# Second pair's k on SyncE, the projection through GpSimd, and a fallback arm without VectorE, in a hash-attention kernel with a channel mix

## The chip, the cores and the metric

The kernel runs on one core of one Trainium2 chip. The metric is the device time of one execution in microseconds (us), as the median of several runs. A profile of one further execution shows what every engine did: PE (TensorE matmuls, with PEld for its weight loads), DVE (VectorE), ACT (ScalarE), POOL (GpSimd) and SP (SyncE, which here only issues transfers). A small q behind an engine's name, as in SPq, means that engine's sequencer: it issues a transfer, waits or branches.

## The reference

Attention comes first, on 4 batches of 8 heads, 768 positions, 64 values a head. Each position of q and k gets six bits, the signs of its products with a 64 x 6 projection; a query attends only to keys with the same six bits.

```python
q_bits = (np.einsum('bhsd,dk->bhsk', q, proj) > 0)
k_bits = (np.einsum('bhsd,dk->bhsk', k, proj) > 0)
mask = q_bucket[:, :, :, None] == k_bucket[:, :, None, :]
scores = np.where(mask, scale * np.matmul(q, k.transpose(0, 1, 3, 2)), -1e9)
attn = softmax(scores)                     # over the keys
x = np.matmul(attn, v)                     # heads side by side: (4, 768, 512)
```

The channel mix follows, with `x_prev` the sequence moved by one position:

```python
xk = mu_k * x + (1 - mu_k) * x_prev
xr = mu_r * x + (1 - mu_r) * x_prev
k = np.maximum(xk @ w_k, 0.0)              # 512 -> 1024
out = sigmoid(xr @ w_r) * ((k * k) @ w_v)  # 1024 -> 512
```

## The kernel before

The program has two arms. The fast arm computes everything under a bound on the size of the scores, and at its end `check_bound` writes an integer `flag` that says whether the bound held. All engines then load this flag (line 1127) and branch (line 1128): if it is zero, `general()` computes everything again in a slower and safer way. With the inputs here the flag holds, and every engine jumps over the general arm. Up to that branch each engine runs the fast arm in the order written in the kernel; a manual schedule keeps it.

The fast arm works on pairs of heads: 16 pairs, and 12 slots for each pair, two heads of six chunks of 128 keys. In each slot `score` (line 454) makes two matmuls, ScalarE takes the exponential (line 461), and two slots later `pv` multiplies the result with the values (lines 473 and 482). Between them stand matmuls of the channel mix (line 551), once a batch of attention is done. Tables named WORK and FETCH say what else is done in which slot.

The part that matters here is the start, before and in the first slots:

- `load_qk(0)` issues the two heads of pair 0's q from SyncE and k from ScalarE (line 249), and behind the first of each a copy of the projection into one half of the tile `projp` (line 254): rows 0 to 63 for one use, rows 64 to 127 for the other.
- A memset and a one-column exponential (line 685) make ScalarE load its table early.
- `load_v(0)` issues pair 0's values on SyncE (line 292), `load_qk(1)` pair 1's q on SyncE and its k on ScalarE (line 259). The second pair's values and pair 2's q and k come later on SyncE, then two small transfers for `mu` (line 721).
- `keep_warm` (line 692) issues matmuls on constants to `idle`, which nobody reads: 9 before the first real work of TensorE and 3 before the sign matmuls.
- `turn_pe` (lines 325 to 329) transposes one head's q or k on TensorE and copies it out of its bank on VectorE or ScalarE; `cast_pe` (lines 337 and 339) makes the bf16 copies for the scores, on GpSimd and ScalarE.
- `bits_first` (line 353) multiplies the projection with the turned q and k of pair 0, and VectorE takes the signs (line 384). Later pairs use `bits_pe` (line 395), whose signs go to their rows by SyncE transfers (line 405).
- `values` (lines 440 to 444) casts and sums values on GpSimd.

Four banks of PSUM go round between the transposes, the sign products and the outputs, by `take` and `give`. A transfer from SyncE or ScalarE signals one of eight semaphores in turn, and a transfer that would use one again waits for the earlier landing on it.

Of the kernel before, what the change touches and what calls it, by code (L numbers as in the profile page):

```python
# [16 lines left out]
P = 128  # L17
# [16 lines left out]
def kernel(  # L34
# [44 lines left out]
    def ffn_mix_unit(pools, b, dc, xt, ms):  # L79
        def u():  # L80
            x = xt[:, P : P + S]
            xp = xt[:, 0:S]
            nc.vector.memset(xt[:, 0:1], 0.0)
            nc.vector.tensor_copy(xt[:, 1:P], xt[:, S : S + P - 1])
            df = pools["df"].tile([P, S], BF16, name=f"df{b}_{dc}", tag="df")
            nc.vector.tensor_tensor(df, x, xp, op=ALU.subtract)
            for i, nm in enumerate(("xk", "xr")):
                m = pools["mix"].tile([P, S], BF16, name=f"{nm}{b}_{dc}", tag="mix")
                nc.vector.tensor_scalar(
                    out=m,  # L90
                    in0=df,
                    scalar1=mu_sb[:, i * NDC + dc : i * NDC + dc + 1],
                    scalar2=None,
                    op0=ALU.mult,
                )
                nc.vector.tensor_tensor(out=m, in0=m, in1=xp, op=ALU.add)
                ms[nm][dc] = m

        return u

    def ffn_k_unit(pools, b, fc, ms):
        def u():
            kp = pools["ps"].tile([P, 2, 512], FP32, name=f"kp{b}_{fc}", tag="sc")
            for dc in range(NDC):
                for sp in range(2):
                    nc.tensor.matmul(
                        kp[:, sp, 0:HALF],
                        wk_sb[:, dc, fc * P : (fc + 1) * P],
                        ms["xk"][dc][:, sp * HALF : (sp + 1) * HALF],
                        start=(dc == 0),  # L110
                        stop=(dc == NDC - 1),
                    )
            kr = pools["kr"].tile([P, 2, HALF], BF16, name=f"kr{b}_{fc}", tag="kr")
            if fc % 2:
                nc.scalar.activation(kr, kp[:, :, 0:HALF], AF.Relu, scale=ROOT_HALF)
            else:
                nc.vector.tensor_scalar(
                    out=kr, in0=kp[:, :, 0:HALF], scalar1=0.0, scalar2=ROOT_HALF,
                    op0=ALU.max, op1=ALU.mult,
                )  # L120
            k2 = pools["k2"].tile([P, 2, HALF], BF16, name=f"k2{b}_{fc}", tag="k2")
            nc.vector.tensor_tensor(out=k2, in0=kr, in1=kr, op=ALU.mult)
            ms["k2"][fc] = k2.rearrange("p s q -> p (s q)")

        return u

    def ffn_vr_unit(pools, b, c, ms):
        def u():
# [9 lines left out]
            for fc in range(NFC):  # L138
# [8 lines left out]
            th = pools["th"].tile([P, DM], BF16, name=f"th{b}_{c}", tag="th")  # L147
            nc.scalar.activation(th, vr[:, 1, :], AF.Tanh, scale=0.5)
            os_ = pools["os"].tile([P, DM], FP32, name=f"os{b}_{c}", tag="os")
            nc.vector.scalar_tensor_tensor(  # L150
                out=os_, in0=th, scalar=1.0, in1=vr[:, 0, :], op0=ALU.add, op1=ALU.mult
            )
# [16 lines left out]
    def fast():  # L169
        with ExitStack() as fx:  # L170
# [39 lines left out]
            KROWS = (slice(0, D + NB), slice(0, P))  # L210
            augs, vas, vss = [], [], []
            for s in range(NSET):
# [8 lines left out]
                for j in range(2):  # L221
                    nc.vector.memset(vas[s][j][:, :, D : D + 1], 1.0)
                    nc.vector.memset(vss[s][j][:, D : D + 1], float(NC_))

# [17 lines left out]
            def load_qk(n):  # L242
# [3 lines left out]
                if n == 0:  # L246
                    for j in range(2):
                        for i, eng in enumerate((nc.sync, nc.scalar)):
# [4 lines left out]
                            if j == 0:  # L253
                                eng.dma_start(
                                    out=projp[ROWS[i], NB * i : NB * i + NB], in_=proj
                                )
                    return
                for i, eng in enumerate((nc.sync, nc.scalar if n == 1 else nc.sync)):
                    eng.dma_start(
                        out=tl[:, i, :, :],  # L260
                        in_=SRC[i][b, 2 * t : 2 * t + 2].rearrange(
                            "j (p c) d -> p j (c d)", c=NC_
                        ),
                    )
# [123 lines left out]
            def bits_pe(n, js):  # L388

                groups = [(j, i) for j in js for i in range(2)]  # L390
                sg = sgp.tile([32 * len(groups), 2, HALF], BF16, name=f"sg{n}_{js[0]}", tag="sg2")
                for e in range(2):
                    which, bb = take([32 * len(groups), HALF], FP32, f"bb{n}_{js[0]}_{e}")
                    for g, (j, i) in enumerate(groups):
                        nc.tensor.matmul(
                            bb[32 * g : 32 * g + 32, :],
                            projp[ROWS[e], NB * e : NB * e + 32],
                            t32(n)[ROWS[e], i, j, :],
                            start=True,
                            stop=True,  # L400
                        )
                    signs(sg[:, e, :], bb)
                    give(which)
                for g, (j, i) in enumerate(groups):
                    nc.sync.dma_start(
                        out=augs[n % NSET]["qk"[i], j][SROWS[j], :],
                        in_=sg[32 * g : 32 * g + NB, :, :].rearrange("r e x -> r (e x)"),
                    )

            def bits_dve(n):  # L410

                which, bb = take([P, HALF], FP32, f"bb{n}")
                strips = [(e, i) for e in range(2) for i in range(2)]
                for g, (e, i) in enumerate(strips):
                    nc.tensor.matmul(  # L415
                        bb[32 * g : 32 * g + 32, :], projp[:, 0:32], t32(n)[:, i, e, :],
                        start=True, stop=True,
                    )
                sg = sgp.tile([P, HALF], BF16, name=f"sg{n}", tag="sg")
                signs(sg, bb)  # L420
                give(which)
                for j in range(2):
                    for g, (e, i) in enumerate(strips):
                        r = 32 * g + NB * j
                        nc.sync.dma_start(
# [259 lines left out]
            nc.scalar.activation(warm, warm, AF.Exp)  # L685
            load_v(0)
            load_qk(1)
# [12 lines left out]
            keep_warm(9, idle[:, 0, 0:HALF])  # L700
# [4 lines left out]
            keep_warm(3, idle[:, 0, 0:HALF])  # L705
# [10 lines left out]
            for i in range(2):  # L716
                cast_pe(0, i, 1, ((nc.gpsimd, nc.scalar), (nc.scalar, nc.gpsimd))[i])
            load_v(1)
            load_qk(2)
# [29 lines left out]
            def turn_mu():  # L749
# [29 lines left out]
                    lambda: bits_pe(1, (0, 1)),  # L779
# [14 lines left out]
                    lambda: bits_pe(2, (0, 1)),  # L794
# [17 lines left out]
                    lambda: bits_pe(3, (0, 1)),  # L812
# [211 lines left out]
    def general_head(nat, work, ps, xt, b, h, j):  # L1024
# [4 lines left out]
        for side, src in (("q", q), ("k", k)):  # L1029
# [10 lines left out]
            if side == "q":  # L1040
                nc.vector.tensor_copy(tv, tp[:, :, 0:HALF])
            else:
                nc.vector.tensor_scalar(
                    out=tv, in0=tp[:, :, 0:HALF], scalar1=0.125, scalar2=None, op0=ALU.mult
                )
            bp = ps.tile([NB, 2, 512], FP32, name=f"gbp{side}{id_}", tag="g2")
            for sp in range(2):
# [7 lines left out]
            nc.vector.tensor_scalar(  # L1055
                out=bt.rearrange("p (s q) -> p s q", s=2),
                in0=bp[:, :, 0:HALF],
                scalar1=0.0,
                scalar2=0.5,
                op0=ALU.is_gt,  # L1060
                op1=ALU.subtract,
            )
            tr[side], bits[side] = t, bt
        ob = work.tile([P, NC_, D], BF16, name=f"gob{id_}", tag="gob")
        for ic in range(NC_):
# [3 lines left out]
            for sp in range(2):  # L1069
# [8 lines left out]
            same = work.tile([P, 2, HALF], FP32, name=f"gsm{id_}_{ic}", tag="gsm")  # L1078
            nc.vector.tensor_scalar(
                out=same, in0=mp[:, :, 0:HALF], scalar1=1.25, scalar2=None, op0=ALU.is_gt  # L1080
            )
            neg = work.tile([P, 2, HALF], FP32, name=f"gng{id_}_{ic}", tag="gng")
            nc.vector.tensor_scalar(
                out=neg, in0=mp[:, :, 0:HALF], scalar1=1.25, scalar2=-1e9, op0=ALU.is_le, op1=ALU.mult
            )
            sm = work.tile([P, 2, HALF], FP32, name=f"gsc{id_}_{ic}", tag="gsc")
            nc.vector.tensor_tensor(out=sm, in0=sp_[:, :, 0:HALF], in1=same, op=ALU.mult)
            nc.vector.tensor_tensor(out=sm, in0=sm, in1=neg, op=ALU.add)
            mx = work.tile([P, 1], FP32, name=f"gmx{id_}_{ic}", tag="gmx")
            nc.vector.tensor_reduce(out=mx, in_=sm, axis=AX.XY, op=ALU.max, negate=True)  # L1090
            pe = work.tile([P, 2, HALF], FP32, name=f"gpe{id_}_{ic}", tag="gpe")
            den = work.tile([P, 1], FP32, name=f"gdn{id_}_{ic}", tag="gdn")
            nc.scalar.activation(pe, sm, AF.Exp, bias=mx, accum_out=den)
# [8 lines left out]
            nc.vector.tensor_copy(pt, tp[:, :, 0:HALF])  # L1102
            op_ = ps.tile([P, D], FP32, name=f"gop{id_}_{ic}", tag="g1")
            for c in range(NC_):
# [6 lines left out]
                )  # L1111
            rc = work.tile([P, 1], FP32, name=f"grc{id_}_{ic}", tag="grc")
            nc.vector.tensor_scalar(out=rc, in0=den, scalar1=1e-9, scalar2=None, op0=ALU.add)
            nc.vector.reciprocal(rc, rc)
            nc.vector.tensor_scalar(
                out=ob[:, ic, :], in0=op_, scalar1=rc, scalar2=None, op0=ALU.mult
            )
        ot = ps.tile([D, NC_, P], BF16, name=f"got{id_}", tag="g1")
        for c in range(NC_):
            nc.tensor.transpose(ot[:, c, :], ob[:, c, :], ident16)  # L1120
        nc.vector.tensor_copy(
# [38 lines left out]
```

## Time and profile before

| what | us |
|---|---|
| median of 3 runs | 254.25 (254.19 to 255.53) |
| the profiled execution | 254.34 |
| its span | 252.5 |
| PE busy | 242.7 (96% of the span) |
| ACT busy | 205.7 (81%) |
| DVE busy | 170.8 (68%) |
| POOL busy | 113.3 (45%) |

The span is the time from the first instruction of the program to the last; the rest of the profiled execution's time lies around it. Rows of the timeline give a start, a duration, the engine, the line of the kernel, the operation, what it writes and reads, and in brackets the idle time before it and what ended it. In the chain of waits, each piece is what released the next.

### The profile page before, as it was taken

Reading aid. Unit: us, or ns where it says so; the run is one execution under the profiler, and the core shown is the slowest. Engines: PE = TensorE matmul, PEld = TensorE weight load, DVE = VectorE, ACT = ScalarE, POOL = GpSimd, SP = SyncE. Lnnn points to the kernel's source line nnn. Section 1 sums busy time; section 2 is a strip of 40 time slices with the busy share of each in tenths; the row PEclk is TensorE's granted clock in tenths of the full one; section 3 lists DMA queues with packets and bytes.
Section 4 is the critical chain, followed back from the end, with each engine's and each line's share of the span. In section 5 each row is a group of like instructions: output and inputs, shape, how many; then the busy total and the mean of one; then the engine's idle time right before and its main releaser. Section 6 shows DMA issues by size and latency. Waiting matters only on the chain.

```text
span 252.5 us, 6670 instructions
## 1 busy us (share of the span) xinstructions
PE 242.7 (96%) x2437; PEld 146.5 (58%) x2437; DVE 170.8 (68%) x397; ACT 205.7 (81%) x334; POOL 113.3 (45%) x214
## 2 busy tenths in 40 slices
PE   8799999899999999999999999999999999999992
PEld 4377766555656555565656555565666565555441
DVE  2588986877888738476888738476888527398431
ACT  3788999999898978889798978889798988649520
POOL 5689688596737270815527270915528000000000
PEclk9999999999999999999999999999999999999998
DMA  6987989296999384847729485757820111110123
GB/s 186 376 181 183 229 162 234 47 222 159 229 176 226 112 195 119 234 114 204 178 74 225 112 194 146 205 117 206 174 66 6 48 42 42 63 66 3 69 100 95
DMA packets 28345, 36.73 MB, mean 145 GB/s; under 512 B 3328, under 2 KB 25488, under 8 KB 28304
## 3 DMA queue, kind: packets, MB, share of 16 engines
q1 hardware_dynamic: 25536, 32.81, 50.6%
q0 software_dynamic: 2128, 2.62, 6.4%
q10 hardware_dynamic: 640, 0.79, 0.9%
q8 instruction: 21, 0.34, 0.6%
q14 instruction: 20, 0.16, 0.3%
HBM read 31.99 MB, written 6.29 MB: 152 GB/s over the span
## 4 chain that ended last, share of the span: by engine, by line
PE 75%; ACT 11%; DMA 7%; issue 3%; SPq 2%; ACTq 0%; DVE 0%
PE sc L454 20%; PE kp L551 16%; PE vp L551 13%; PE oo L482 10%; ACT pt L461 8%; PE rp L551 7%; PE bb L415 3%; DMA qk<-in_k_dram 3%; DMA out_dram<-os 2%; DMA bl<-in_k_dram 2%; PE tp L325 2%; PE oo L473 2%; SPq L278 2%; PE ot L511 1%; ACT sq L308 1%
## 5 line engine op out<-in xcount | busy, mean ns | idle before, releaser
L461 ACT ACTIVATE pt<-sc 128x768 bf16<-128x768 f32 x192 | 151.1, 813 | 21.3 <-PE sc L454 19.2
L454 PE MATMUL sc<-aq,ak 70*128 70x384 bf16 (+1 forms) x384 | 94.0, 325 | 2.6 <-ACT pt L461 1.5
L482 PEld LDWEIGHTS <-pt 128*128 128x128 bf16 x1152 | 60.5, 97 | 26.8 <-ACT pt L461 0.9
L482 PE MATMUL oo<-va,pt 128*128 128x65 bf16 x1152 | 66.3, 193 | 0.1
L551 PE MATMUL vp<-wv_sb,k 128*128 128x512 bf16 (+1 forms) x200 | 54.3, 370 | 0.0
L551 PE MATMUL kp<-xk,wk_sb 128*128 128x384 bf16 x256 | 52.6, 326 | 0.0
L454 PEld LDWEIGHTS <-ak 70*128 70x128 bf16 (+1 forms) x384 | 34.5, 97 | 28.9 <-issue 7.6
L374 POOL TENSOR_SCALAR aq<-t 64x768 bf16<-64x768 f32 x24 | 19.8, 826 | 63.1 <-DVE t L369 49.4
L588 DVE TENSOR_TENSOR k<-kr 128x384 bf16<-128x384 bf16 x64 | 26.9, 430 | 9.6 <-ACT kr L582 8.9
L609 DVE SCALAR_TENSOR_TENSOR os<-th,vp 128x512 f32<-128x512 bf16 (+1 forms) x25 | 16.6, 665 | 20.1 <-PE vp L551 18.1
L551 PEld LDWEIGHTS <-wk_sb 128*128 128x128 bf16 x256 | 21.6, 97 | 13.6 <-issue 3.8
L551 PE MATMUL rp<-wr_sb,xr 128*128 128x512 bf16 x96 | 27.7, 379 | 0.0
L582 ACT ACTIVATE kr<-kp 128x384 bf16<-128x384 f32 x41 | 20.4, 496 | 4.4 <-PE kp L551 4.4
L551 PEld LDWEIGHTS <-k 128*128 128x128 bf16 x200 | 16.8, 97 | 10.8 <-issue 1.2
L369 DVE STREAM_TRANSPOSE t<-bl 128x768 f32<-128x768 f32 x24 | 22.3, 957 | 0.0
L374 POOL TENSOR_SCALAR ak<-t 64x768 bf16<-64x768 f32 x24 | 20.1, 839 | 4.8 <-DVE t L369 3.1
L599 ACT ACTIVATE th<-rp 128x512 bf16<-128x512 f32 x24 | 14.2, 592 | 9.7 <-PE rp L551 9.7
L308 ACT ACTIVATE sq<-bl 128x768 bf16<-128x768 f32 x24 | 20.2, 841 | 0.0
L512 DVE COPY xt<-ot 128x768 bf16<-128x768 bf16 x16 | 8.9, 558 | 15.9 <-PE ot L511 15.9
L442 POOL TENSOR_TENSOR s<-vf 128x192 f32<-128x192 f32 x32 | 19.6, 612 | 0.0
L494 DVE SCALAR_TENSOR_TENSOR ob<-oo,rc 128x384 bf16<-128x384 f32 x32 | 17.8, 557 | 1.1
L440 POOL CAST va<-vf 128x384 bf16<-128x384 f32 x32 | 16.8, 526 | 2.5 <-DMA vf<-in_v_dram 1.4
(69 smaller groups left out, 224.2 us busy)
## 6 DMA issues: line engine op xcount, KB each, us to landing
bl<-in_q_dram SPq DMA_DIRECT2D x48, 176.0 KB
bl<-in_k_dram SPq DMA_DIRECT2D x48, 176.0 KB
vf<-in_v_dram SPq DMA_DIRECT2D x16, 384.0 KB
out_dram<-os SPq DMA_DIRECT2D x18, 256.0 KB
out_dram<-os SPq DMA_DIRECT2D x12, 128.0 KB
qk<-in_q_dram SPq DMA_DIRECT2D x3, 384.0 KB
wk_sb<-in_moe_w_k_dram POOLq DMA_DIRECT2D x2, 512.0 KB, 6.7
wv_sb<-in_moe_w_v_dram POOLq DMA_DIRECT2D x2, 512.0 KB, 9.0
```

What stands on the lines that cost most here:

```text
L308: nc.scalar.activation(junk, src, AF.Square, accum_out=acc)
L369: nc.vector.transpose(t32(n)[:, i].rearrange("p h (c f x) -> p (h c) f x", c=3, f=4), src)
L374: eng.tensor_scalar(out=augs[n % NSET]["qk"[i], j][ROWS[j], :], in0=t32(n)[ROWS[j], i].rearrange("p h y -> p (h y)"), scalar1=(1.0, ALPHA)[i],
L440: nc.gpsimd.tensor_copy(to, of)
L442: nc.gpsimd.tensor_add(s3, vf[:, 0 : 3 * D], vf[:, 3 * D : 6 * D])
L454: nc.tensor.matmul(sc[:, sp, 0:HALF], au["k", j][kr, jc * P : (jc + 1) * P], au["q", j][kr, sp * HALF : (sp + 1) * HALF], start=True, stop ...
L461: nc.scalar.activation(pt.rearrange("p (s q) -> p s q", s=2), sc[:, :, 0:HALF], AF.Exp, bias=EXP_BIAS, scale=SCALE,)
L482: nc.tensor.matmul(oo[:, ic, :], pts[n, j, jc][:, ic * P : (ic + 1) * P], vas[n % NSET][j][:, jc, :], start=False, stop=(jc == NC_ - 1 and ...
L494: nc.vector.scalar_tensor_tensor(out=obs[n][:, :, j * D : (j + 1) * D], in0=oo[:, :, 0:D], scalar=ROOT_HALF, in1=rc.to_broadcast([P, NC_, D]),
L551: nc.tensor.matmul(box["t"], lhs(), rhs(), start=(i == 0), stop=(i == len(mms) - 1))
L582: nc.scalar.activation(kr, kp, AF.Relu)
L588: 1, lambda: nc.vector.tensor_tensor(out=k2, in0=kr, in1=kr, op=ALU.mult)
```

## The change

- `load_qk`: the projection goes to `projp` by one GpSimd transfer, issued before GpSimd's memsets, into rows 0 to 63; GpSimd copies it to rows 64 to 127 behind those memsets. The two projection transfers on SyncE and ScalarE go.
- `load_qk(1)` issues both q and k on SyncE, and stands ahead of `load_v(0)`; `load_qk(2)` stands ahead of `load_v(1)`.
- `keep_warm` has 8 and 2 matmuls instead of 9 and 3.
- `bits_pe` is split into two calls, one for each half `e` of the positions. The instructions that it gives stand in the same order on every engine as before; `BY_GPSIMD` is empty, so its transfers stay on SyncE.
- The general arm, with the functions `ffn_mix_unit`, `ffn_k_unit`, `ffn_vr_unit` and `general_head`, uses GpSimd and ScalarE where it used VectorE, with longer sequences where GpSimd can't do the same in one step. VectorE has no instruction left in it.

Up to the branch, VectorE's order is the same as before. TensorE has two constant matmuls fewer; ScalarE has the projection transfer and pair 1's k fewer; GpSimd has one transfer and one copy more.

The diff, cut to its core (of the general arm a few lines stand for all):

```diff
@@ ffn_k_unit (general arm)
-            if fc % 2:
-                nc.scalar.activation(kr, kp[:, :, 0:HALF], AF.Relu, scale=ROOT_HALF)
-            else:
-                nc.vector.tensor_scalar(
-                    out=kr, in0=kp[:, :, 0:HALF], scalar1=0.0, scalar2=ROOT_HALF,
-                    op0=ALU.max, op1=ALU.mult,
-                )
+            nc.scalar.activation(kr, kp[:, :, 0:HALF], AF.Relu, scale=ROOT_HALF)
             k2 = pools["k2"].tile([P, 2, HALF], BF16, name=f"k2{b}_{fc}", tag="k2")
-            nc.vector.tensor_tensor(out=k2, in0=kr, in1=kr, op=ALU.mult)
+            nc.gpsimd.tensor_tensor(out=k2, in0=kr, in1=kr, op=ALU.mult)
...
@@ fast
             KROWS = (slice(0, D + NB), slice(0, P))
+            nc.gpsimd.dma_start(out=projp[0:D, 0:NB], in_=proj)
             augs, vas, vss = [], [], []
...
                     nc.vector.memset(vss[s][j][:, D : D + 1], float(NC_))
+            nc.gpsimd.tensor_copy(projp[D:P, NB : 2 * NB], projp[0:D, 0:NB])
...
@@ load_qk
-                            if j == 0:
-                                eng.dma_start(
-                                    out=projp[ROWS[i], NB * i : NB * i + NB], in_=proj
-                                )
                     return
-                for i, eng in enumerate((nc.sync, nc.scalar if n == 1 else nc.sync)):
-                    eng.dma_start(
+                for i in range(2):
+                    nc.sync.dma_start(
...
+            load_qk(1)
             load_v(0)
-            load_qk(1)
...
-            keep_warm(9, idle[:, 0, 0:HALF])
+            keep_warm(8, idle[:, 0, 0:HALF])
...
-            keep_warm(3, idle[:, 0, 0:HALF])
+            keep_warm(2, idle[:, 0, 0:HALF])
...
+            load_qk(2)
             load_v(1)
-            load_qk(2)
...
-                    lambda: bits_pe(1, (0, 1)),
+                    lambda: bits_pe(1, 0),
+                    lambda: bits_pe(1, 1),
...
@@ general_head
-            nc.vector.tensor_copy(pt, tp[:, :, 0:HALF])
+            nc.scalar.copy(pt, tp[:, :, 0:HALF])
...
```

## The prediction

> **What bounds the kernel now.** I read the busy lines first, then the chain of waits over the first 30 us, then PE's waits, then who waited at the very end.
>
> ```profile
> PE 242.7 (96%) x2437; PEld 146.5 (58%) x2437; DVE 170.8 (68%) x397; ACT 205.7 (81%) x334; POOL 113.3 (45%) x214
> ```
>
> PE is busy 96% of the span, so only 10 us are not matmuls. The change touches nothing that the middle runs (no matmul, activation or vector operation there is added or dropped), so what it can win lies in those 10 us. From the chain of waits (start, duration, what):
>
> ```profile
> 2.42 1.28 ACT L685
> 3.72 0.20 ACT warm L685
> ...
> 3.93 7.55 DMA qk<-in_k_dram
> ...
> 11.62 0.52 PE tp L325 x3
> ```
>
> Pair 1's k is issued by ScalarE, behind a projection transfer, the table load and the warm-up activation, at 3.93; it lands at 11.48. PE's waits say what that costs (us in total, times, longest):
>
> ```profile
> PE tp L325 <- DMA qk<-in_k_dram: 1.1, 1, 1.1
> ```
>
> Every other wait of PE after 9 us is 0.3 us or less, and from 11.62 the chain is PE's until 33 us, ScalarE's exponentials to 55, then almost all PE's. A start that comes earlier is therefore carried to the end, unless an engine or a load that does not move with it becomes the late one. The rows around the hole:
>
> ```profile
> 10.06 0.49 PE L454 MATMUL sc<-aq,ak 70*128 70x384 bf16 x2
> 10.27 0.48 ACT L329 COPY t<-tp 128x384 f32<-128x384 f32 x1
> 10.64 0.82 ACT L461 ACTIVATE pt<-sc 128x768 bf16<-128x768 f32 x1
> 11.62 0.52 PE L325 MATMUL tp<-ident,qk 128*128 128x128 f32 x3 [1.06 <-DMA qk<-in_k_dram]
> 12.17 0.48 ACT L329 COPY t<-tp 128x384 f32<-128x384 f32 x1 [0.72 <-PE tp L325]
> 12.96 0.33 PE L473 MATMUL oo<-vs,epsm 128*128 128x390 bf16 x1
> ```
>
> The other end: PE's last matmul ends near 247.7 and VectorE's last operation at 248.2, yet the span is 252.5. The waits of SyncE in the last 3.5 us, and the rows of line 1128 (the If):
>
> ```profile
> SPq L1155 <- DVEq L1128: 1.3, 1, 1.3
> ```
> ```profile
> L1128 DVEq COMPARE_BRANCH x1: 72/72/72, 248.6 to 248.6; - x1
> L1128 SPq COMPARE_BRANCH x1: 50/50/50, 249.4 to 249.4; - x1
> L1128 ACTq EVENT_SEMAPHORE  x1: 17/17/17, 250.3 to 250.3; - x1
> L1128 PEldq EVENT_SEMAPHORE  x1: 51/51/51, 250.4 to 250.4; - x1
> L1128 DVEq EVENT_SEMAPHORE  x1: 21/21/21, 251.4 to 251.4; - x1
> ```
>
> The flag says that the general arm is not needed, and each engine jumps over its part of it. VectorE branches at 248.6 and does its next instruction at 251.4, 2.8 us later. SyncE, with no instruction in the arm, branches at 249.4 and its next stands at 249.6. SyncE's closing waits end with VectorE's semaphore, and the final barrier follows.
>
> **The head, part by part.** SyncE loses its projection transfer (0.60 us at 1.21) and gains pair 1's k behind pair 1's q; ScalarE loses a projection (0.56) and the k (0.39). The second heads' q and k are then issued at about 1.2 instead of 1.80 and 1.86, and nothing small lies between large transfers. With the moved rate between 3.15 and 4.65 us at 63 to 236 GB/s, and 350 to 390 from 5 us on, the stream has a hole there that goes. Bytes to the end of pair 1's k: 4 x 197 KB + 2 x 393 KB = 1.57 MB; at 370 GB/s from 2.1 us that is 6.4, with the spread of landings (1.5 us for pair 1's q) at most 8. PE needs it at 10.4. So the wait goes whole; it would still go if the rate stayed at today's.
>
> What is late next? PE's two score matmuls start 0.16 apart at 10.06, so the next transpose can start at 10.39: 11.62 - 10.39 = 1.23 us, the upper bound. ScalarE limits it: its exponential ends at 11.46, the copy of that transpose starts at 11.36 (it overlaps by 0.1, as the one at 13.25 does) and ends at 11.84, and the first output matmul takes the bank that this copy frees: 11.90 instead of 12.96, 1.06 us. The third exponential moves only 0.8 (lower bound), but ScalarE later idles 0.42 us before its sixth, for PE, so it catches up. I take 1.1.
>
> Pair 0's values now land behind k: 1.97 MB, at 7.4 by the same rate, against GpSimd's cast waiting until 7.89; at worst 8.3. GpSimd is dense from there to 27.2 and so does not move with PE. Its deadlines after a move of 1.1: the first sums (9.74) at 11.9; pair 1's keys (15.04) at 20.67 - 1.1 = 19.6. The cover is 2 us or more, so this costs nothing; a values landing 2 us late would cost what exceeds it. Pair 1's values move behind pair 2's q and k: by the bytes they land near 10.8, about as now. SyncE's later queue (block loads, sign rows) keeps its order.
>
> The fillers fall from 9 and 3 to 8 and 2. PE's first real transpose at 3.92 waits for pair 0's q, landing at 3.7, not for the ninth filler; the sign matmuls (5.91) wait for ScalarE's copy that ends at 5.92, not for the twelfth. Nothing won or lost, as long as the clock rises as now (below).
>
> **The projection through GpSimd.** GpSimd finishes its identities at 1.66 and issues one transfer; the weights' issues on that queue cost 0.79 to 0.93. Behind it stand four memsets (4 x 0.36, done by 4.1, first needed after 14 us), then the copy to the upper half, which waits for the landing, then the casts that now start at 5.45 for VectorE's copy. The landing is not in this trace. Below: the same 1.5 KB from the other queues reached PE's use 2.9 to 3.7 us after issue, so 4.6 to 5.4. Above: the five weight transfers on this queue, 512 KB each, took 5.6 to 9.1. In size it is nearest to the first; I take 4.9, the copy 0.3 (the 128x64 rows of GpSimd take 0.32), ready at 5.2. The sign matmuls need it at 5.9: free, with 0.7 us of cover. The Trainium skill (DMA: Bandwidth & Descriptors, "Anatomy of one DMA — SWDGE (gpsimd) path") gives 2.0 us fixed plus bytes over 436 GB/s, by which it would land at 3.7; for 512 KB the rule gives 3.2, and the weight rows here took 5.6 and more.
>
> **The tail.** The general arm without VectorE leaves VectorE's flag load and branch and takes away what it jumps over; the nearest row is SyncE's 0.2 us. Its semaphore then stands at 248.9 and is no longer last. Next is the last output's landing, 251.09 by the trace's semaphore records. Two hardware transfers fewer also turn the eight semaphores on which the trace records landings by two places, so SyncE has two more waits of 0.07 behind the last landing. Drain at 251.3 instead of 251.65: 0.33, or 0.47 without these waits. A freed fetch in the final microseconds may hasten the last rows: 0.9 at most (250.77, the transfer before). Lower bound 0, if VectorE still stalls. I take 0.4. The Trainium skill (Runtime: NRT & Kernel Launch, "Instruction fetch mechanics") says that a taken branch out of the two-page window forces a fetch; by that, the lower bound is left only for a page that ends just there, and the 0.2 us of SyncE agrees. ScalarE and GpSimd get longer arms, but they jump as now, at 250.3 and 240.7.
>
> Sum against the profiled run's own time of 254.34 (span 252.5, 1.8 around it; 0.09 above the median of 254.25): -1.1 - 0.4 = 252.84, by the median 252.75. I say 252.8.
>
> **The rivals.** One half fails. Tail only (ScalarE or GpSimd keeps the head): 253.9. Head only, because the change does not do what it says there and VectorE still stalls at the branch: 253.2. For it speaks that its flag load alone took 0.7 us; against it SyncE's row. Together 0.17.
>
> Slower: the projection is late. It decides from a landing of 5.6 on; head and tail gains are spent at a landing of 7.2 (5.6 + 1.23 + 0.4). With the median of the weight rows, 7.7 after issue, it lands at 9.3, the sign matmuls start at 9.65 instead of 5.91, all behind them is 3.7 late, the 1.23 of the old wait is absorbed: +2.5 - 0.4 = 256.4. For: the same queue's rows, and its first use. Against: 4 pieces for each of 16 engines instead of 512 KB. 0.09.
>
> The clock. PE's fillers are 0.32 us apart at first and 0.16 from about 5.5 us, 4.4 us after the first. With 8 fillers PE stands idle 0.3 us near 3.6. If the step came 4.4 us later, what PE does on the path up to 9.9 us would take twice as long: the first part of the sign matmuls (0.4), a score (0.3), the second signs (0.8) and a transpose (0.4), +1.9: 252.84 + 1.9 = 254.7. The Trainium skill (TensorE: Matmul & The Clock Gate, Part 1) has a free-running window of about 3.4 us that must be busy; by that rule a 0.3 us gap could cost one window, and this trace shows no such case. 0.08; a second miss would pass 256.
>
> **How the numbers follow.** Both gains: 0.66, own range 252.2 to 253.3. One of them: 0.17. Late projection or clock: 0.17, of which 0.12 beyond 255.5. Half a percent, 1.27 us, is about what a measurement of this kernel can tell from no change: faster means below 252.98, which holds for 0.55 of the 0.66. The rest of it, the halves and 0.05 of the slow cases are within: 0.33. Slower 0.12. The range to 254.4 takes in the halves; 252.2 is 1.23 + 0.9 off.
>
> **What would show it.** Right: no wait of PE on pair 1's k, first output matmul near 11.9, sign matmuls still at 5.9, VectorE's semaphore at line of the If 0.2 us behind its branch, SyncE's last wait on an output. Wrong: the sign matmuls waiting for GpSimd, 0.32 us matmuls beyond 5.5 us, or a VectorE gap of 2.8 us after the branch.

## The result, and the profile after

The changed kernel takes 255.73 us (median of 20 executions, 253.88 to 258.09), the kernel before 254.29 beside it: ratio 1.0054, with a 95% interval of 1.0029 to 1.0078. In a second comparison it was 255.97 against 254.42, ratio 1.0065 (1.0036 to 1.0093). It is slower by 0.5 to 0.65%, where the forecast said 252.8 and a gain. (A ratio leaves out single executions more than 1.5% above the fastest of their kernel; a median counts all.)

| | before | after |
|---|---|---|
| profiled execution, us | 254.34 | 255.92 |
| its span | 252.5 | 253.2 |
| outside the span, profiled execution | 1.84 | 2.72 |
| outside the span, median | 1.84 | 2.49 |

PE's work is the same but for the two constant matmuls. The trace after holds 24 matmuls fewer than the one before, of which 22 are records that it lacks (a second profile of the same kernel, after_ref, has 2435):

```profile
PE 241.4 (95%) x2413; PEld 146.0 (58%) x2435; DVE 170.6 (67%) x397; ACT 205.5 (81%) x334; POOL 113.6 (45%) x216
```

PE's waits in the first 60 us (us in total, times, longest):

```profile
PE sc L468 <- DMA ak<-sg: 1.1, 1, 1.1
PE idle L706 <- DVE epsm L68: 1.1, 1, 1.1
PE bf L349 <- DMA projp<-in_proj_dram: 1.1, 1, 1.1
```

The wait for pair 1's k is gone, as forecast. Two others of the same length stand there instead: for the projection (`bits_first`, now line 349), and for the sign rows of pair 2 (`score`, now line 468). The sign rows are the rows of q and k that take the signs, brought there by small SyncE transfers. The chain of waits up to 34 us (start, duration, what) runs through both:

```profile
1.67 5.28 DMA projp<-in_proj_dram
...
7.08 1.10 PE bf L349 x8
...
20.82 4.49 DMA bl<-in_k_dram
25.32 6.69 DMA ak<-sg
32.01 0.09 issue
32.10 0.48 PE sc L468 x2
```

And the rows of the timeline at the head (start, duration, engine, line, operation, idle time before it):

```profile
7.08 1.07 PE L349 MATMUL bf<-t,projp 64*32 64x384 f32 x8 [1.05 <-DMA projp<-in_proj_dram]
7.08 0.18 POOL L223 COPY projp<-projp 64x6 f32<-64x6 f32 x1 [3.14 <-DMA projp<-in_proj_dram]
...
10.65 0.81 ACT L475 ACTIVATE pt<-sc 128x768 bf16<-128x768 f32 x1
...
13.21 0.34 PE L487 MATMUL oo<-vs,epsm 128*128 128x390 bf16 x1
```

GpSimd's transfer is issued at 1.67 and lands at 6.95, not at 4.9. The sign matmuls start at 7.08 instead of 5.92, the first exponential 1.09 later than before. The absent wait for k takes most of this back: the 17th exponential is only 0.16 late. Then come the sign rows. They were issued at 25.32, 0.52 later than before, on SyncE's queue behind eight block loads of 176 KB, and landed at 32.01. Before, they were issued at 24.80 and landed at 30.40, for a use at 30.68, with 0.28 us to spare; the rows of before:

```profile
24.80 0.68 SPq L405 DMA_DIRECT2D ak<-sg  x1
...
30.68 0.49 PE L454 MATMUL sc<-aq,ak 70*128 70x384 bf16 x2
```

So 0.52 of the 1.61 came from the later issue, and 1.09 from a transfer that took 6.69 us instead of 5.60. From the 33rd exponential on everything is 1.35 late, to the end of PE (1.32). This is one execution. In after_ref's profile the rows landed at 30.90, PE stood idle 0.35 there, and it ended 0.22 after that of before.

The other end. SyncE's closing waits, and VectorE's rows at the If (line 1170) and at the end (1197):

```profile
SPq L1197 <- DMA out_dram<-os: 1.1, 4, 0.3
SPq L1197 <- PEq L1197: 0.7, 2, 0.5
```
```profile
L1170 DVEq COMPARE_BRANCH  x1: 72/72/72, 249.9 to 249.9; - x1
```
```profile
L1197 DVEq DRAIN  x2: 10/14/17, 250.1 to 252.6; - x2
```

VectorE goes on 0.2 us behind its branch, not 2.8, and SyncE no longer waits for it. So the span grew by 0.65 (its last rows) where PE ended 1.32 later. But the time outside the span, taken as constant, grew by 0.88 in this execution. The sum, 1.32 - 0.67 + 0.88 = 1.53, is the 1.58 between the two profiled executions but for rounding.

### The profile page after: what moved, and what is told of

Its sections match the earlier page's. It is cut to its first block, busy times and chain, and to the rows that moved or that the text cites. A ratio compares the mean times of both kernels' runs of the same rounds, so it can differ in the third digit from the quotient of the medians.

```text
span 253.2 us, 6646 instructions
## 1 busy us (share of the span) xinstructions
PE 241.4 (95%) x2413; PEld 146.0 (58%) x2435; DVE 170.6 (67%) x397; ACT 205.5 (81%) x334; POOL 113.6 (45%) x216
## 3 DMA queue, kind: packets, MB, share of 16 engines
HBM read 31.99 MB, written 6.29 MB: 151 GB/s over the span
## 4 chain that ended last, share of the span: by engine, by line
PE 64%; ACT 12%; DMA 10%; issue 5%; SPq 3%; POOL 3%; DVE 2%; ACTq 0%; POOLq 0%
PE sc L468 16%; PE kp L565 15%; PE vp L565 12%; ACT pt L475 9%; PE oo L496 8%; PE rp L565 6%; DMA out_dram<-os 3%; PE bb L427 3%; DMA ak<-sg 3%; SPq L274 2%; DMA projp<-in_proj_dram 2%; ACT sq L304 2%; DMA bl<-in_k_dram 2%; PE oo L487 1%; PE ot L525 1%
## 5 line engine op out<-in xcount | busy, mean ns | idle before, releaser
L565 PE MATMUL vp<-wv_sb,k 128*128 128x512 bf16 (+1 forms) x184 | 50.4, 369 | 0.6
L565 PE MATMUL rp<-wr_sb,xr 128*128 128x512 bf16 x90 | 26.8, 379 | 0.3
```

The lines of the kernel that those rows point to most:

```text
L565: nc.tensor.matmul(box["t"], lhs(), rhs(), start=(i == 0), stop=(i == len(mms) - 1))
```

## Experiments

Three questions: which half costs, why the projection costs more than its wait, and what the arm is worth. "Before" is the kernel before, on the same chip in the same comparison; span and the time outside it are medians too, of the executions that the ratio counts.

| kernel | median | before | ratio (95%) | span | outside |
|---|---|---|---|---|---|
| arm_only | 255.55 | 254.51 | 1.0016 (0.9984 to 1.0047) | 253.7 | 1.83 |
| fast_only | 255.41 | 254.51 | 1.0021 (0.9985 to 1.0056) | 253.4 | 1.77 |
| proj_hw | 253.57 | 254.51 | 0.9936 (0.9904 to 0.9968) | 250.9 | 2.75 |
| rows_first | 255.09 | 254.51 | 1.0009 (0.9976 to 1.0043) | 252.7 | 2.42 |
| hw_oldarm | 253.68 | 254.62 | 0.9968 (0.9951 to 0.9984) | 251.8 | 1.87 |
| hw_vfirst | 253.23 | 254.62 | 0.9951 (0.9931 to 0.9970) | 250.6 | 2.64 |
| gp_only | 254.79 | 254.62 | 1.0013 (0.9994 to 1.0031) | 252.9 | 1.81 |
| gp_early | 255.02 | 254.62 | 1.0006 (0.9983 to 1.0029) | 252.3 | 2.54 |
| after_cover | 254.77 | 254.87 | 0.9974 (0.9947 to 1.0001) | 252.8 | 1.94 |
| vfirst_oldarm | 253.51 | 254.87 | 0.9938 (0.9912 to 0.9964) | 251.6 | 1.83 |
| gp_early2 | 254.59 | 254.87 | 0.9972 (0.9939 to 1.0005) | 252.2 | 2.44 |
| k_only | 254.12 | 254.87 | 0.9974 (0.9942 to 1.0005) | 252.2 | 1.86 |
| after_ref | 255.97 | 254.42 | 1.0065 (1.0036 to 1.0093) | 253.5 | 2.42 |
| cover_rows | 254.00 | 254.42 | 0.9977 (0.9956 to 0.9998) | 251.9 | 1.92 |
| vfirst_new | 253.32 | 254.42 | 0.9943 (0.9917 to 0.9968) | 250.7 | 2.72 |
| vfirst_old | 253.68 | 254.42 | 0.9949 (0.9924 to 0.9974) | 251.8 | 1.82 |
| after_nofill | 256.83 | 254.29 | 1.0056 (1.0019 to 1.0092) | 254.3 | 2.40 |
| vfirst_warm | 254.36 | 254.29 | 0.9994 (0.9969 to 1.0019) | 252.6 | 1.87 |

### The parts alone

**arm_only** is the kernel before with the new general arm alone; **fast_only** is the changed kernel with the old arm.

> The kernel before, with the general arm of the changed kernel and nothing else of it. Theory A (what the arm wins at VectorE's branch is given back after the span): the span falls by 0.4 to 0.7 us, the time outside the span grows from 1.8 to about 2.6 us, and the time stays within 0.4 us of the kernel before. Rival B (the arm is a plain gain of 0.4 us, as forecast): the time outside stays 1.8, time 253.9 against 254.3. Rival C (the longer arms of ScalarE and GpSimd are what made the kernel slower): 1 us or more slower.

> The changed kernel with the general arm of the kernel before, so only the start is changed. Theory A (the start costs 1.3 us by pair 2, the arm nothing): span about 253.9, time outside 1.8, time about 1.3 us above before, as the whole change. Rival C (the arm costs): within 0.4 us of before.

Neither interval excludes 1, so neither half alone can be called the loss, though both medians lie about 1 us above before. arm_only missed its expectation: its span did not fall, and the time outside it stayed at 1.83. Its profile says where the gain at VectorE's branch went. VectorE is no longer waited for; SyncE's last wait is on TensorE's sequencer:

```profile
SPq L1176 <- PEq L1176: 2.4, 2, 2.2
```

In the kernel before this wait is 0.7 in total, 0.5 at the longest. After the final release at 250.73 TensorE goes on only at 252.78; the last blocks of instructions were fetched from 250.26 and 250.46 on and had landed by 251.45. That the wait is for such a fetch is argued, not shown, and 1.3 us of it come after the landing.

The profile of arm_only also shows how far two profiles of one head differ: nothing in its head is changed, and yet PE's wait for k is 0.65 instead of 1.06, and PE ends 0.30 earlier. Between the two profiles of the changed kernel PE's end differs by 1.1. The ends of PE given below are of single profiles and have to be read with this in mind; the times are medians.

### The projection back on the hardware queues

**proj_hw**: the changed kernel with the two projection transfers of before. **hw_oldarm**: the same with the old general arm. **k_only**: the kernel before with only pair 1's k moved.

```diff
@@ proj_hw, against the changed kernel
-            nc.gpsimd.dma_start(out=projp[0:D, 0:NB], in_=proj)
-            nc.gpsimd.tensor_copy(projp[D:P, NB : 2 * NB], projp[0:D, 0:NB])
+                            if j == 0:
+                                eng.dma_start(
+                                    out=projp[ROWS[i], NB * i : NB * i + NB], in_=proj
+                                )
@@ k_only, against the kernel before
-                for i, eng in enumerate((nc.sync, nc.scalar if n == 1 else nc.sync)):
-                    eng.dma_start(
+                for i in range(2):
+                    nc.sync.dma_start(
```

> The changed kernel with the projection as before, by one transfer on SyncE and one on ScalarE behind the first q and k. Theory A (GpSimd's transfer, 5.3 us from issue to landing, holds the sign matmuls by 1.2 us and eats the gain on pair 1's k): the sign matmuls start at 5.9, PE does not wait for pair 1's k, the first output matmul stands near 11.9 instead of 13.2. If pair 2's sign rows move with the start, the time is 2.4 us below the changed kernel, about 253.3; if they land near 31 us whatever the start does, only 1.2 to 1.4 us, about 254.4. Rival D (the order of the large transfers is what costs): the sign matmuls at 5.9, but a later first output matmul than 12.9.

> The changed kernel with the projection back on SyncE and ScalarE, and with the general arm of before: only the order of the loads is new. Theory (the new arm is worth nothing outside the branch itself; what VectorE saves inside the span comes back after it): the time equals that of proj_hw, 253.6 within 0.3, with 1.8 us outside the span instead of 2.75, and with VectorE's 2.8 us behind its branch. Rival (the arm is worth the 0.4 us forecast): 254.0 or more. Rival (the arm costs, as the 0.4 us of arm_only hint): 253.2 or less. In the head: PE waits 0.9 us for pair 0's values, none for k or the projection.

> The kernel before with one edit: pair 1's k is issued by SyncE, directly behind pair 1's q. Values, projection, fillers and general arm are as before. Theory (the wait for this k is the one gain of the changed order): k lands near 10.4, a wait of at most 0.2 us is left, PE's end moves 0.8 to 1.0 us, 253.6 to 253.8. Rival (only k ahead of the values lands in time): a wait of 0.5 us or more is left, 254.1 or more.

This settles the main point: with the projection on SyncE and ScalarE the kernel is 0.3% (old arm) to 0.6% (new arm) faster than before; on GpSimd it is 0.5 to 0.65% slower with the new arm, and 0.2% with the old one (fast_only, not clear of 1, but its interval lies above that of hw_oldarm). The head alone (hw_oldarm) gives 0.94 of the 1.1 forecast. In k_only a wait of 0.5 is left on k, as its rival said, and PE ends 0.49 earlier; the time points the same way, with an interval that just reaches 1. (In hw_vfirst and vfirst_new below, k lies behind the values again and there is no wait on it, so the 0.5 is not the price of that order alone.) In proj_hw the projection landed at 3.93 and 5.01, but PE's waits show two small ones that the forecast had ruled out:

```profile
PE oo L489 <- POOL vs L460: 0.9, 1, 0.9
...
PE sc L470 <- DMA ak<-sg: 0.2, 1, 0.2
```

The second is the sign rows of pair 2. The first is pair 0's values, now behind pair 1's k: GpSimd's cast waits for them until 10.31, and the first sums are late.

```profile
10.31 0.51 POOL L456 CAST va<-vf 128x384 bf16<-128x384 f32 x1 [4.14 <-DMA vf<-in_v_dram]
...
12.21 0.33 PE L489 MATMUL oo<-vs,epsm 128*128 128x390 bf16 x1 [0.90 <-POOL vs L460]
```

### The projection through GpSimd: alone, and issued earlier

**gp_only**: the kernel before with the projection through GpSimd and nothing else. **gp_early** and **gp_early2**: the changed kernel with that transfer ahead of the identities, in gp_early2 with the memset of its tile on GpSimd.

```diff
@@ gp_early2, against the changed kernel
+    projp = consts.tile([P, 64], FP32, name="projp")
+    nc.gpsimd.memset(projp, 0.0)
+    nc.gpsimd.dma_start(out=projp[0:D, 0:NB], in_=proj)
     ident32 = consts.tile([P, P], FP32, name="ident32")
...
-    projp = consts.tile([P, 64], FP32, name="projp")
-    nc.vector.memset(projp, 0.0)
...
-            nc.gpsimd.dma_start(out=projp[0:D, 0:NB], in_=proj)
```

> The kernel before with one edit: the projection by one GpSimd transfer and a copy. Theory (the late projection is the main cause of the loss): landing 5.3 us or more after the issue, so after 6.9; the sign matmuls near 7.1 instead of 5.91 and the first exponential 1.1 us later; the wait for pair 1's k absorbs most of it, since k still lands at 11.5, so the end moves by 0.1 to 0.4 only: 254.4 to 254.7, with a wider scatter than before. Rival (the transfer is late only because the changed order puts more bulk ahead of it): landing at 5.5 or earlier, time as before. Rival (the delay is carried to the end whole): 255.4.

> The changed kernel with GpSimd's projection transfer issued ahead of the identities, about 1 us earlier. Theory A (a transfer on this queue has a latency of its own of some 5.3 us): it lands near 6.0, the sign matmuls start near 6.2, the first exponential is 0.2 to 0.3 us later than before instead of 1.1; the sign rows of pair 2 are issued earlier too, so of the 1.1 us wait on them 0.2 to 0.6 is left: 254.3 to 255.0. Theory B (its packets move only when the hardware queues let up): it lands near 6.9 all the same, and the time is that of the changed kernel, 255.7.

> The changed kernel with GpSimd's projection transfer ahead of the identities, and the memset of its tile on GpSimd too, so that the issue does not wait for VectorE as it did in gp_early: issue near 0.9 instead of 1.67. Theory A (the transfer has a latency of its own of 5.3 us): landing near 6.2, a wait of PE of 0.2 to 0.4, mean clock 0.995 or more in nearly all executions, about 254.5. Theory B (its packets move only when the first hardware transfers are through, near 5.1): landing near 6.9 whatever the issue, a wait of 1 us or more, 255.5.

In gp_only the projection is as late as in the changed kernel (PE waits 1.5 us, sign matmuls at 6.78), and the wait for k swallows it: PE ends 0.1 earlier than before, and the time is that of before within its interval. So a late projection does not make the kernel slower where the wait for k still stands. The two early kernels did not test what they were made for. The issue moved only from 1.67 to 1.52 and 1.34, and the landings, 6.76 and 6.42, lie 5.24 and 5.08 behind it. Over the profiles with the issue at 1.66 or 1.67 the landing went from 6.29 to 6.95. In the changed kernel its 16 packets start to move between 5.16 and 6.38, so 3.5 of the 5.28 us passed before the first. Whether this delay belongs to the queue or to the bulk transfers beside it stays open.

gp_early showed something else. Its sign matmuls took 1.73 us for eight where the changed kernel took 1.07, and its next six transposes 1.54 instead of 0.88:

```profile
6.89 1.73 PE L349 MATMUL bf<-t,projp 64*32 64x384 f32 x8 [0.64 <-DMA projp<-in_proj_dram]
...
8.55 1.54 PE L321 MATMUL tp<-ident,qk 128*128 128x128 f32 x6
```

Its granted clock first steps up at 10.44, against 5.46 in the kernel before.

### The clock and the sign rows

**rows_first**: the changed kernel with pair 5's k blocks issued behind pair 2's sign rows. **after_cover**: with 10 constant matmuls instead of 2 ahead of the sign matmuls. **cover_rows**: both. **after_nofill**: with none. **after_ref**: the changed kernel as it is.

```diff
@@ rows_first
-                (0, 10): (
-                    lambda: load_pair(5, "k"),
-                ),
...
+                (1, 2): (
+                    lambda: load_pair(5, "k"),
+                ),
@@ after_cover (after_nofill leaves the line out)
-            keep_warm(2, idle[:, 0, 0:HALF])
+            keep_warm(10, idle[:, 0, 0:HALF])
```

> The changed kernel with pair 5's k blocks issued in slot (1, 2) instead of (0, 10), so that four block loads of 176 KB no longer stand ahead of pair 2's sign rows on SyncE. Theory A (the rows land behind the blocks, 6.7 us after issue): the rows land 2 us or more sooner, PE's wait of 1.1 us on them near 31 us goes, and the time is 1.1 us below the changed kernel, about 254.6. Rival E (the rows are late because the start is late, or for another reason than the blocks): the wait stays, 255.7.

> The changed kernel with 10 constant matmuls instead of 2 ahead of the sign matmuls, so that TensorE works through its wait for the projection. Theory (that idle wait costs twice: once as a wait, and in about half of the executions once more, since the granted clock then is at half for 3.4 us): no execution with a mean granted clock of 0.993 or less, none above 256.5, and a median near 254.9. Rival (the clock drops for a reason that has nothing to do with the wait, and the scatter is that of the landing): clocks of 0.984 to 0.993 in half of the executions, and 255.7 as in the changed kernel.

> The changed kernel as it is, as the measure for cover_rows. Theory (three costs: wait for the projection, half clock in about half of the executions, sign rows): ratio to before 1.002 to 1.007, a third to a half of the executions with a mean granted clock of 0.993 or less, and those 1.5 to 2.2 us above the rest. Rival (the clock has no part in it): as many low clocks as in the kernel before.

> The changed kernel with 10 constant matmuls instead of 2 ahead of the sign matmuls, and pair 5's k blocks issued behind pair 2's sign rows. Theory (the clock and the sign rows carry most of the loss, and the late projection itself is absorbed where the wait for pair 1's k had stood): no low clock, no wait on sign rows, PE's end within 0.2 of before, 0.2 to 0.4 below before and 1.2 to 1.8 below after_ref. Rival (the wait itself is carried to the end): 0.5 us or more above before.

> The changed kernel without the 2 constant matmuls ahead of the sign matmuls. No real work moves, and the idle wait of TensorE for the projection becomes 0.4 to 0.8 us longer. Theory (the idleness itself costs, since the granted clock then stays or falls to half for 3.4 us in part of the executions): 0.3 to 1.2 us slower than the changed kernel, 256.2 to 257, ratio to before 1.008 to 1.012, and half or more of the executions with sign matmuls at half speed or a mean clock of 0.993 or less. Rival (only the landing counts): 255.7 to 256.0, ratio 1.0054 to 1.0065.

In the profile of rows_first the wait on the sign rows is gone, but PE stands idle 2.0 us for the projection, and then the clock is gone too; its median, 255.09, lies above the 254.6 expected. The windows of 1 us (for PE, PEld, VectorE, ScalarE and GpSimd the busy time and in brackets the instructions, then the granted clock, DMA share, GB/s):

```profile
5.00:6.00 1.00, 0.01 (x1) 0.00 (x0) 0.00 (x0) 0.97 (x3) 0.00 (x0) 1.00 0.96 201
6.00:7.00 1.00, 0.00 (x0) 0.02 (x1) 0.00 (x0) 0.16 (x1) 0.00 (x0) 1.00 0.93 324
7.00:8.00 1.00, 0.99 (x8) 0.34 (x8) 0.00 (x0) 0.00 (x0) 0.89 (x3) 0.60 1.05 392
8.00:9.00 1.00, 1.00 (x8) 0.33 (x3) 0.21 (x1) 0.00 (x0) 0.29 (x1) 0.50 1.05 389
9.00:10.00 1.00, 1.00 (x6) 0.81 (x4) 0.95 (x3) 0.39 (x1) 0.12 (x1) 0.50 1.07 386
10.00:11.00 1.00, 0.98 (x8) 0.36 (x10) 0.97 (x2) 0.81 (x3) 0.94 (x2) 0.70 1.07 376
```

The clock had stepped up at 3.78, fell to half at 7.20 and came back at 10.61, steps of 3.41 us; the first exponential was 2.29 later than before, although the projection landed no later than in the changed kernel. The Trainium skill (TensorE: Matmul & The Clock Gate, Part 1) describes such a gate, half rate after an idle window of about 3.4 us and full rate after a busy one; the trace agrees with the period, and it shows a fall after 2.0 us without a matmul.

The mean granted clock of an execution shows such falls: 3.41 us at half rate take 0.7% off it, while the idle end of the kernel alone takes it to 0.994 at the lowest profile without a fall (vfirst_oldarm). An execution at 0.993 or less is therefore likely to hold a fall. There are 31 of 92 in the seven comparisons of kernels with the changed head's projection through GpSimd and 0 or 2 constant matmuls ahead of the sign matmuls, 0 of 24 with 10 of them, 0 of 91 with the changed order of loads, or k's part of it, and the projection on the hardware queues. The kernel before has it too, in 15 of 158, and arm_only in 2 of 12. A late projection does not bring it about each time: gp_early2, one of the seven, has 0 of 12, and gp_only has 0 of 12, with waits of 1.4 and 1.5 us in their profiles. In the changed kernel (both comparisons) the 13 executions at 0.993 or less have a median of 256.98, the 19 others 255.32 (in after_ref alone the two lie 1.1 apart, where 1.5 to 2.2 was expected). The count is a lower bound: gp_early, at half speed until 10.44, is recorded with 1.0, as the record starts with the first step. In after_cover PE has no wait on the projection or on sign rows, and the sign matmuls run at full rate from the start:

```profile
5.37 1.89 PE L706 MATMUL idle<-epsm 128*128 128x384 bf16 x10
7.18 0.85 PE L349 MATMUL bf<-t,projp 64*32 64x384 f32 x8
```

They start 0.1 later than in the changed kernel, and still cover_rows takes 254.00 against 255.97 for after_ref in the same comparison, with 0.23% less than before (interval just below 1). Of these 1.97 us, 1.6 lie in the span and 0.5 outside it. after_nofill, with no real work moved, has a median of 256.83, 2.5 above before, and half of its executions are at 0.993 or less. But its ratio, which leaves out 3 of the 12, is 1.0056, that of the changed kernel and of its rival; 1.008 to 1.012 was expected. That a longer idle time makes the kernel slower is therefore not shown by its time. What a fall costs is shown by its profile: the first exponential is as late as in the changed kernel, 1.11 after that of before, but with the clock at half from 8.29 to 15.12 the 17th is 2.26 late instead of 0.16. The second sign matmuls of after_nofill, and then of the changed kernel:

```profile
10.17 1.51 PE L349 MATMUL bf<-t,projp 64*32 64x384 f32 x8
```
```profile
10.23 0.85 PE L349 MATMUL bf<-t,projp 64*32 64x384 f32 x8
```

So a fall of the clock costs about 2 us where it comes. How much of the 1.97 is the clock's and how much the sign rows' is not settled: after_cover and rows_first each hold a part, in comparisons of their own, and an earlier start also issues the sign rows earlier.

### The values first, and the arm side by side

**hw_vfirst**: proj_hw with `load_v(0)` ahead of `load_qk(1)`, and with the edit of rows_first. **vfirst_oldarm**: the same with the old arm. **vfirst_new** and **vfirst_old** are these two again, in one comparison. **vfirst_warm**: hw_vfirst with 9 and 3 constant matmuls.

```diff
@@ hw_vfirst, against proj_hw (and rows_first's edit)
-            load_qk(1)
             load_v(0)
+            load_qk(1)
```

> The changed kernel with the projection back on the hardware queues, pair 0's values issued ahead of pair 1's q and k, and the k blocks of pair 5 issued behind the sign rows of pair 2. Theory (values and sign rows are the two waits that ate the head's gain in proj_hw): no wait of PE on the values, on k or on sign rows; PE's end moves 1.0 to 1.2 us ahead of before instead of 0.6; 0.4 to 0.5 us below proj_hw, near 253.1. Rival (k, behind the values again, lands too late): k lands after 10.4 and the wait of 1 us on it is back, 253.6 or more.

> hw_vfirst with the general arm of before. Theory (the new arm takes 1.0 to 1.2 us out of the span and gives 0.8 back after it): span near 251.7 instead of 250.6, 1.85 us outside it instead of 2.64, 253.5 in all, 0.2 to 0.5 above hw_vfirst. Rival (the arm is worth nothing, and the 0.45 us between hw_oldarm and hw_vfirst are those of the values and the sign rows): 253.2, equal to hw_vfirst. Rival (the arm costs): below 252.9.

> hw_vfirst again, beside its twin with the general arm of before. Theory (the arm takes 1.0 us out of the span and gives 0.7 to 0.8 back after it): 253.2, with 0.2 to 0.3 us less than vfirst_old. Rival (all of the gain is given back): equal within 0.1.

> vfirst_oldarm again, beside hw_vfirst: 253.5, with 1.85 us outside the span against 2.6 for its twin; by the rival 253.2 to 253.3.

> hw_vfirst with 9 and 3 constant matmuls as before, instead of 8 and 2. Theory (without the late projection the shorter runs cost and gain nothing): 253.2 to 253.4, ratio 0.994 to 0.995. Rival (they are worth their own 0.16 to 0.32 us each on the path): 253.6; rival (more constant matmuls bring the clock up sooner): 252.8 or less.

No wait on values or k is left; hw_vfirst's profile still has 0.3 on the projection and 0.3 on the sign rows, vfirst_new's has neither. PE ends 1.03 (hw_vfirst) and 1.66 (vfirst_new) before the kernel before. The medians are the lowest of all, 253.23 and 253.32, with ratios of 0.9951 and 0.9943; by the ratios proj_hw (0.9936) and vfirst_oldarm (0.9938) can't be told from them.

The arm: in one comparison the median is 253.32 with the new one and 253.68 with the old (ratios 0.9943 and 0.9949, with intervals that overlap almost wholly). The other pair, 253.23 and 253.51, was measured in two comparisons, and its ratios point the other way (0.9951 and 0.9938). A gain of about 0.3 us from the arm is possible, and not shown. The span is 1.0 to 1.1 shorter, the time outside it 0.8 to 0.9 longer. SyncE's closing waits, vfirst_old and then vfirst_new:

```profile
SPq L1178 <- DVEq L1151: 1.8, 1, 1.8
```
```profile
SPq L1199 <- PEq L1199: 0.7, 2, 0.5
SPq L1199 <- DMA out_dram<-os: 0.4, 2, 0.3
```

vfirst_warm missed all its expectations. Its PE ends 1.28 before that of the kernel before, so the constant matmuls are neutral at the head, but the time is 254.36. The end took it back, as in arm_only:

```profile
SPq L1199 <- PEq L1199: 2.1, 2, 1.9
```

With the new arm, then, the tail changes with the number of constant matmuls that TensorE has; the changed kernel against after_cover, and vfirst_new against vfirst_warm, differ in nothing else. With 12 (arm_only, vfirst_warm) TensorE holds the last barrier for about 2 us inside the span, and 1.8 to 1.9 lie outside. With 8 to 10 it does not, but 2.4 to 2.8 lie outside. With 18 (after_cover, cover_rows) it does not, and 1.9 lie outside. The number shifts TensorE's code, so a fetch of its last block may be the reason (in the trace of the changed kernel a block of instructions is fetched at 255.37, behind the span); no run isolated it. A version with hw_vfirst's loads and 18 constant matmuls wasn't tried.

## Why the prediction was wrong, point by point

- **The wait for pair 1's k** (-1.1): right. It went, and with the projection where it was the head is worth 0.94 (hw_oldarm).
- **The projection "ready at 5.2: free, with 0.7 us of cover"**: the step that failed first. The size was wrong: the transfer took 5.28 us, not 3.2, landed at 6.95, and the sign matmuls waited for it until 7.08; with the projection back on its old queues the kernel is faster than before. The rows of like size, on the other queues, were the wrong ones to go by; the weight rows of the same queue, 5.6 and more, came nearer and were kept only as the upper end. The 0.3 us for the copy was not on the path: the sign matmuls start beside it, at 7.08. By the rule of the Trainium skill (DMA: Bandwidth & Descriptors, "Anatomy of one DMA — SWDGE (gpsimd) path") it would have landed at 3.7; the measured 6.95 decides. The rival of a late projection, by its own slope, gives 252.84 + 6.95 - 5.6 = 254.2 at that landing. That rival was the right mechanism, with too low a chance, and by this reckoning it holds about half of the miss. The trace agrees: the 1.1 not won, and 0.16 besides, at the 17th exponential.
- **The fillers, "nothing won or lost, as long as the clock rises as now"**: failed through its condition. The two rivals were priced apart, but they can be one event: a late projection is idle time in which the clock can fall, or stay at half. rows_first, gp_early and after_nofill show it in their rows, after_cover the reverse. It comes in a part of the executions, and the 1.9 put on it is near the 1.7 between the two medians above.
- **"SyncE's later queue keeps its order"**: true, and beside the point. The sign rows of pair 2 had 0.28 us to spare in the trace of before; they were a deadline not looked up, and stand behind 1.4 MB on their queue. The sum put them at nothing; they cost 1.1 in the profiled execution, 0.35 in after_ref's.
- **The values, "cover is 2 us or more"**: wrong. They landed at 9.59 in the changed kernel, where the late projection hid it, and at 10.26 in proj_hw, against 8.3 "at worst"; there it is a wait of 0.9.
- **The tail** (-0.4): right inside the span, -0.67 with VectorE's gap gone as stated. The step that failed is "1.8 around it", taken as a constant: 2.49 in the median. What was left of the gain is 0.36 in the medians of vfirst_new and vfirst_old, and not clear of noise.

## What to carry to other kernels

A transfer that gates the first real work is better priced from rows of its own queue than from rows of its size on another; and when it comes late, TensorE's idle time can be paid a second time in the clock, so cover it with matmuls that nobody needs or move the transfer. When a start is moved, look up the slack of every later transfer on the same queue, the small ones behind bulk above all. A tail gain has to be read from the time of the whole execution, not from the span.

## What the runs showed of the hardware that was not expected

- 1.5 KB through GpSimd's queue took 4.6 to 5.3 us from issue to landing in these profiles, the same through SyncE and ScalarE 2.7 to 4.4 (3.8 in proj_hw, 4.4 in hw_vfirst).
- The granted clock fell to half after 2.0 us without a matmul, for 3.41 us (rows_first); in after_nofill, after a wait of 1.66, it was at half from 8.29 to 15.12. In every trace the steps of the clock lie a multiple of 3.41 us apart (5.46 to 251.22 in the kernel before: 72 of them).
- With the new arm the time outside the span went from 1.8 to between 1.8 and 2.8, with the number of TensorE's instructions.
